# Two more score steps ahead of the outputs in each row of a burst, three sums of w_out by DMA, and a new list of shifts and engines, in a lightning-attention and feed-forward kernel

## The chip, the cores and the metric

One NeuronCore of a Trainium2 chip runs the whole program. The metric is device time in microseconds, the median of several runs of the same program. PE is the matrix engine (PEld is its loading of weights, which overlaps its products), DVE, ACT and POOL are the three engines for elementwise work, SP is the engine that here only issues DMAs. PE writes to PSUM, of which there are eight banks; DVE and ACT read it, POOL does not here.

## The reference

Attention with a decaying state, over four batches, eight heads, 768 positions and a head size of 64, in blocks of 64 positions; then a feed-forward network with SiLU over all 3072 tokens (512 to 2048 and back).

```python
Dmask = np.where(rel >= 0, lam[:, None, None] ** rel[None, :, :], 0.0)
for b in range(nb):
    qb, kb, vb = (q[:, :, sl], k[:, :, sl], v[:, :, sl])
    intra = np.einsum('bhic,bhjc->bhij', qb, kb) * Dmask[None]
    intra = np.einsum('bhij,bhjd->bhid', intra, vb)
    inter = np.einsum('bhid,bhde->bhie', qb * lam_pow[None], kv_state)
    out[:, :, sl] = intra + inter
    kb_dec = kb * rev_pow[None]
    kv_state = lam_block[None, :, None, None] * kv_state + np.einsum('bhsd,bhse->bhde', kb_dec, vb)
...
h = x @ w_in
g = h * (1.0 / (1.0 + np.exp(-h)))
return (g @ w_out)
```

## The kernel before

**Units.** The kernel works on blocks of 128 positions of one batch (24 units, all eight heads at once); two units make a pair, so there are 12 pairs (numbered 0 to 11), three to a batch. For a pair, `load_pair` (L432) fetches k, q and v as three transfers of 512 KB into `raw`; `prepare` casts k and q to bf16 (`kq`, four casts in pairs 4 to 11, of 64 partitions each), scales v by powers of lambda (`vd`), and turns `kq` to `kqT`, by PE in pairs 0 to 3 (L578) and by a transposing DMA on SP's queue (L593) from pair 4 on. `attention` makes the states (`y`, `xf`, and `xs_all`/`xe_all` as bf16 copies that PE can read) and the masks over the scores (`st`).

**Bursts.** From pair 3 on the small matmuls of a pair are issued in one burst, made of 64x64 tiles of the PE array; a matmul in the upper row of tiles and one in the lower run side by side, and the function `burst` keeps a list for each row (0 and 1) and merges the two by estimated time. A burst of pair n holds up to four kinds of step: the **states' terms** of pair n-1 (L633, `inter64`: queries times the carried state), the **states** of pair n (L659, "d", one chunk at a time in each row), the **scores** of pair n (L670, "s"), and the **outputs** of pair n-1 (L626, "o": masked scores times v). States, scores and outputs have eight steps in each row (four pairs of heads, two halves), of two matmuls each; the states' terms have four in each row. Outputs are added in PSUM to the states' terms, which went to the same banks from other rows of the array; so ahead of the first output stands a fence (`fence(at_inter)`): a `nop` of PE that waits until the last of the states' terms is done. In the kernel before, the order in a burst that has both a new and an old pair is: row 0: states' terms, states (chunk 0), outputs, scores; row 1: states' terms, four score steps, outputs, states (chunk 1, unless the pair ends a batch), the other four score steps. The burst is cut into three parts (after the last output, after the last score of the first two pairs of heads, end), so that DVE can start the evacuation `xt` and the masks `st` early. Bursts of pairs 5 to 11 have both an old pair that is in `CROSSED` and a new one.

**Feed-forward.** `product1` (L935) multiplies a group of units with w_in, ACT applies SiLU (L951, `g`), and `product2` (L977) multiplies by w_out for units 0 to 11. Units 12 to 23 go in fours: `product2_of_four` (L1126) uses a seven-product scheme for 2x2 blocks, and so does `product1_of_four` (L1254) for the fours from units 16 and 20. These need sums of quarters: of `g` (`asum`, tag "a"; some by a copy on SP's queue, L1107, and an accumulating DMA on POOL's queue, L1113), of w_out (`bsum`, tag "b", made by `sums_of_w_out` from five pairs of quarters, two halves each), of x (`xsum`) and of w_in (`wsum`, tag "w"). `bsum` and `wsum` live in slots of the pool `raw` (13 slots), as do the loads.

**The order of everything.** Nothing is issued in the order of the program text. Each piece of work is added to a `Planner` as a task with a key, costs by engine that may do it, dependencies and buffers; the planner plays the program forward with these costs, takes on each free engine the ready task with the lowest key whose buffers are free, and the tasks are then issued in the resulting order, which on each engine is fixed from then on. Keys are about twice the pair's number; loads have keys from -100 up, transposes -150 up, the copies for `bsum` by DMA would have `TKEY + i / 4 - 2` (i is the place in the dictionary `SEVEN`, whose order is 3, 4, 5, 1, 2, 7, 6) with `TKEY` 9. Two dictionaries adjust it: `SHIFT` adds to the key of a task or of a family of tasks (by its tag: `('first', 6)` are all first products of group 6), and `HOME` pins a task to one engine. Among the constants, `AWAY` lists the pairs whose casts and scalings may also go to POOL, and `BMOVED` the products whose sums of w_out are made by DMA: a copy of 512 KB on SP's queue (`put`) and an accumulating DMA of 512 KB on POOL's (`more`), in place of two additions on DVE or POOL. Up to 19 us, gaps on PE are filled with products of `ones` (L1321).

Of the kernel before, what the change touches and what calls it, by code (L numbers as in the profile page):

```python
# [39 lines left out]
def names_of(tag):  # L40


    if not isinstance(tag, tuple):
        return tag, None, None
    kind, n = tag[:2]
    if kind in ("cast", "scale", "burst", "mask", "y", "xe", "xf", "xt"):
        whole = "pair", n
    elif kind in ("first", "silu", "x", "to u", "u2", "u3", "h12", "h22"):
        whole = "group", n
    elif kind in ("seven", "a", "a copy", "to P", "to B", "to R", "on R", "m3", "c11", "c12", "c21", "c22"):  # L50
        whole = "four", n
    else:
        whole = None
    return tag, tag[:2] if len(tag) > 2 else None, whole


class Planner:
# [5 lines left out]
    BEGIN = {"PE": 0.8, "ACT": 5.6, "DVE": 2.7, "POOL": 3.4, "SP": 0.8}  # L63
    SWITCH = 0.095

    SHIFT = {('cast', 10, 1, 0): -0.5, ('cast', 10, 1, 1): -2.5, ('cast', 6): -3.5, ('cast', 7, 1, 0): -1.5, ('first', 2): -0.5,
             ('first', 2, 6): -8, ('first', 3, 6): -8.5, ('first', 4, 4): 1, ('first', 5, 0): -4, ('first', 5, 6): -0.5,
             ('first', 6): 6.25, ('first', 6, 11): 2.25, ('first', 6, 12): -1, ('first', 6, 14): 13.25, ('first', 6, 15): 2.25,
             ('first', 6, 2): 0.5, ('first', 6, 3): 0.25, ('first', 6, 4): -4.5, ('first', 6, 5): -10.75, ('first', 7): -0.25,
             ('first', 7, 0, 4): 1.75, ('first', 7, 1, 4): 1, ('first', 7, 2, 3): 1, ('first', 8, 0, 5): -4,  # L70
             ('first', 8, 1, 1): -3.5, ('first', 8, 2, 4): 4.5, ('four', 12): 4.5, ('four', 20): -0.75, ('group', 2): 0.25,
             ('group', 3): -5.5, ('group', 7): 4.75, ('group', 8): -7.5, ('load w', 3, 1): -1.5, ('mask', 11): 5.75, ('mask', 5): 3,
             ('mask', 7, 0, 1): 3, ('mask', 8, 0, 0): 5.75, ('mask', 9, 0, 1): 0.25, ('outputs', 0, 0): 4, ('pair', 10): 2.5,
             ('pair', 11): -9.75, ('pair', 4): -7.5, ('pair', 5): -0.75, ('pair', 9): 8.75, ('scale', 3, 0): -1, ('score', 1): 8,
             ('second', 10): 7, ('seven', 12): 0.5, ('seven', 12, 3): -8.25, ('seven', 12, 5): -4.75, ('seven', 16): 3.75,
             ('seven', 20): 3.75, ('silu', 8, 1, 0, 1): 2.75, ('states', 2, 0): 6.75, ('store', 9): -2, ('turn', 3, 0, 1): -10.75,
             ('turned', 1): -7.25, ('u3', 8): 5.5, ('w', 1): 6.75, ('xe', 0, 0, 1): 4.5, ('xe', 11): 11.75, ('xe', 3, 0, 0): 1.5,
             ('xf', 6): -10.25, ('xt', 7, 1): 7, ('y', 10, 0, 0): 5.75}
    HOME = {('a', 16, 1, 1): 'POOL', ('a', 20, 5, 0): 'POOL', ('a', 20, 5, 1): 'POOL', ('b', 3, 1): 'POOL',
            ('cast', 11, 1, 1): 'POOL', ('cast', 3, 0, 1): 'ACT', ('cast', 4, 0, 0): 'DVE', ('cast', 5, 0, 0): 'POOL',  # L80
            ('cast', 5, 1, 0): 'POOL', ('cast', 5, 1, 1): 'ACT', ('cast', 6, 0, 0): 'DVE', ('cast', 6, 1, 0): 'DVE',
            ('cast', 6, 1, 1): 'ACT', ('cast', 7, 1, 0): 'DVE', ('cast', 7, 1, 1): 'ACT', ('cast', 8, 1, 1): 'DVE',
            ('cast', 9, 0, 0): 'POOL', ('cast', 9, 1, 0): 'POOL', ('cast o', 1, 1): 'DVE', ('cast o', 2, 0): 'ACT',
            ('cast o', 2, 1): 'ACT', ('cast w', 1, 3): 'POOL', ('m3', 12): 'DVE', ('result', 1): 'ACT', ('scale', 11, 0): 'POOL',
            ('scale', 9, 0): 'POOL', ('to u', 7, 3): 'DVE', ('turned', 0, 0, 1): 'DVE', ('turned', 0, 1, 0): 'ACT',
            ('u3', 8, 0): 'DVE', ('u3', 8, 1): 'ACT', ('u3', 8, 2): 'ACT', ('w', 3, 0): 'POOL', ('w', 4, 0): 'POOL',
            ('x', 7, 3): 'POOL', ('x', 8, 1): 'POOL', ('xe', 6, 0, 0): 'POOL', ('xe', 6, 0, 1): 'POOL', ('xe', 7, 0, 0): 'ACT',
            ('xf', 10, 0, 1): 'POOL', ('xf', 4, 0, 1): 'DVE', ('xf', 7, 0, 0): 'POOL'}
    FIRST, LAST, AHEAD = {"SP": 1.15, "ACT": 1.15, "POOL": 1.0}, 1.0, 0.75

    def __init__(self, pools, becomes):
# [5 lines left out]
    def add(self, key, on, fn, deps=(), bufs=(), nbytes=0, kind=None, prior=(), late=0.0, tag=None, lock=False):  # L97
        key = key if isinstance(key, tuple) else (key,)
        key = (key[0] + sum(self.SHIFT.get(n, 0.0) for n in names_of(tag) if n is not None),) + key[1:]
        if tag in self.HOME:  # L100
            on = {self.HOME[tag]: on[self.HOME[tag]]}
        t = Task(key, on, fn, deps, list(bufs), nbytes, kind, prior, late)
# [183 lines left out]
def kernel(  # L286
# [11 lines left out]
    B, H, S, D = q.shape  # L298
# [4 lines left out]
    NP = H // 2  # L303
# [3 lines left out]
    EARLY = 4  # L307
    FINE = (0,)
    TIED, SOLO, CROSSED = 3, (3,), range(4, 12)
    AWAY, XAWAY, OWN = range(5,12), (), (0, 1)  # L310
    PORT = 3
    SMALL = (0, 1)
    OKEY = 0.0
    WKEY, WCAST, WON = -2.0, {"POOL": 0.75, "ACT": 0.62, "DVE": 0.45}, [("POOL", "ACT", "DVE")] * 2 + [("POOL", "DVE"), ("POOL", "ACT")]
    FIRST_ONES, ONES_UNTIL = 10, 19.0
    BMOVED, POOLED = (), (6,)
    LOADED, MOVED, HEAD = (4, 9), (12,16), (1.8, 1.8, 1.2, 0.6)
    TKEY, SEVENS, LAG, WSKEY, FIRST_SEVENS = 9.0, 12, 5.0, 14.0, (16,20)

    ctx.enter_context(tc.manual_schedule())  # L320
    const = ctx.enter_context(tc.tile_pool(name="const", bufs=1))
# [157 lines left out]
    xt = [Buf(f"xt{len(us)}") for us in groups]  # L479
# [123 lines left out]
    def burst(n, alone=False):  # L603
# [3 lines left out]
        o, new = dict(last_pair), n < NU // 2 and not alone  # L607
# [38 lines left out]
        if new:  # L646
            kq, kqT, vd, ck, cv, turned, kq_of, t_of = ready_of[n]
# [28 lines left out]
        def queue(row, what, width, fn, *more, part=slice(None)):  # L676
            rows[row].extend([(what, 0.0005 + 0.00044 * width, lambda a=(k, r) + more: fn(*a), k) for k, r in steps][part])
# [2 lines left out]
            queue(0, "d", 64, state, 0)  # L680
        if o:

            ahead = NP if new and o["n"] in CROSSED else 0
            if new:
                queue(1, "s", 128, score, 1, part=slice(ahead))
            queue(0, "o", 128, output, 0)
            queue(1, "o", 128, output, 1)
        elif new:
            queue(1, "s", 128, score, 1)
        if new:  # L690
            if not final:
                queue(1, "d", 64, state, 1)
            queue(0, "s", 128, score, 0)
            if o:
                queue(1, "s", 128, score, 1, part=slice(ahead, None))
        order, at = [], [0.0, 0.0]
        while rows[0] or rows[1]:
            c = 0 if rows[0] and (not rows[1] or at[0] <= at[1] + 1e-9) else 1
            what, w, f, k = rows[c].pop(0)
# [30 lines left out]
    def attention(n):  # L730
# [10 lines left out]
        if tied:  # L741
            if n - 1 in SOLO:
                burst(n, True)
            buf, sts, bursts = burst(n)
            de = bursts[1]
# [556 lines left out]
    for n in range(NU // 2):  # L1302
        attention(n)
    burst(NU // 2)
    if FIRST_SEVENS:
        sums_of_w_in()
# [17 lines left out]
    ends, first = {}, {}  # L1324
# [9 lines left out]
    def vacant(a, z):  # L1334

        best = None
        for b in {(b.pool, b.slot): b for _, b in first.values()}.values():
            spans = sorted(lives[b.pool, b.slot])
            if all(end + 0.3 < a or start >= z - 1e-6 for start, end in spans):
                nxt = min([start for start, _ in spans if start >= z - 1e-6], default=1e9)  # L1340
                if best is None or nxt < best[0]:
                    best = nxt, b
        return best and best[1]

    at = 0.0
    for start, _, e, t in planned:
        if e == "PE":
            if not at:
                occupy(vacant(0.5, start), FIRST_ONES, 512)
            elif start < ONES_UNTIL and start - at > 0.15:  # L1350
                b = vacant(at, start)
# [34 lines left out]
```

## Time and profile before

| what | value |
|---|---|
| median of 3 runs (lowest, highest) | 205.16 us (204.65, 205.41) |
| the profiled execution, whole | 204.5 us |
| its span, first to last instruction | 202.8 us |
| granted PE clock, mean | 0.998 |
| L935 PE, first products | 67.4 us busy, 448 matmuls |
| L977 PE, second products | 49.6 us busy, 192 matmuls |
| casts to kq: DVE, ACT, POOL | 18, 17 and 13 in pairs 4 to 11 |
| bsum additions on DVE | 9 of 128x1024, mean 1081 ns |
| bsum additions on POOL | 1, 2549 ns |

The span is what the profiler sees between the first and the last instruction; the device time has some 1.7 us more around it. Busy time of PE includes the pipelined ends of its matmuls; the spacing of their starts tells how fast PE really runs. The trace shows the first products from 16.52 us on, without a break from 17.93 us; the first burst at 39.26 us and the last at 143.54 us; the last matmul ends at 199.67 us.

### The profile page before, as it was taken

The page shows a single profiled execution, that of the slowest core. Times are in us where ns is not written, and L with a number is a line of the kernel's source. Part 1 is how long each engine was busy: PE and PEld are TensorE (multiplying, and loading weights), DVE is VectorE, ACT ScalarE, POOL GpSimd, SP SyncE. Part 2 cuts the span into 40 slices and gives each one's busy share as a digit, 9 for nine tenths or more (in the row PEclk, how much of TensorE's full clock was granted, in tenths as well). Part 3 has the DMA queues.
Part 4 walks back from the last instruction along what each step waited for, and adds up shares of the span by engine and source line. Part 5 has one row for each costly group of instructions (what it writes and reads, how often), then busy time and mean ns, then how long its engine had stood idle before and what let it go on. Part 6 is the DMA issues. An engine that isn't in the chain of part 4 may idle for free.

```text
span 202.8 us, 6082 instructions
## 1 busy us (share of the span) xinstructions
PE 196.8 (97%) x2585; PEld 145.3 (72%) x2585; DVE 146.2 (72%) x231; ACT 123.4 (61%) x193; POOL 71.4 (35%) x84
## 2 busy tenths in 40 slices
PE   6999999999999999999999999999999999999993
PEld 2776887867865557557776465458888888888882
DVE  3697749778994949599795875969765766743972
ACT  3697887849785655705384626683796878564010
POOL 4105430222560400058766041338954372000800
PEclk9999999999999999999999999999999999999999
DMA  4999999999999999899999471119997967111324
GB/s 110 339 335 366 386 362 334 368 313 382 230 282 261 318 344 298 208 311 218 303 255 213 130 128 33 57 58 222 176 184 184 218 179 136 52 55 52 107 103 155
DMA packets 71658, 44.43 MB, mean 219 GB/s; under 512 B 18448, under 2 KB 64528, under 8 KB 71632
## 3 DMA queue, kind: packets, MB, share of 16 engines
q1 hardware_dynamic: 62400, 34.74, 62.4%
q0 software_dynamic: 5456, 4.46, 14.4%
q10 hardware_dynamic: 3776, 4.86, 7.2%
q8 instruction: 20, 0.33, 0.6%
q14 instruction: 6, 0.05, 0.1%
HBM read 27.27 MB, written 6.29 MB: 165 GB/s over the span
## 4 chain that ended last, share of the span: by engine, by line
PE 90%; DVE 5%; issue 2%; ACT 1%; ACTq 0%
PE banks L935 27%; PE banks L1126 18%; PE banks L977 17%; PE banks L1254 12%; PE banks L1321 4%; PE banks L626 2%; PE banks L670 2%; PE banks L578 2%; DVE kq L409 1%; DVE xt L414 1%; PE banks L633 1%; DVE st L414 1%; PE banks L659 1%; PE banks L848 1%; PE banks L898 1%
## 5 line engine op out<-in xcount | busy, mean ns | idle before, releaser
L935 PE MATMUL banks<-xt,w_in_bf 128*128 128x256 bf16 (+1 forms) x448 | 67.4, 288 | 0.4 <-DVE xt L414 0.2
L951 ACT ACTIVATE g<-banks 128x512 bf16<-128x512 f32 x64 | 46.0, 745 | 26.8 <-PE banks L935 25.4
L935 PEld LDWEIGHTS <-w_in_bf 128*128 128x128 bf16 x448 | 42.9, 98 | 15.3 <-issue 0.8
L977 PE MATMUL banks<-w_out_bf,g 128*128 128x512 bf16 x192 | 49.6, 379 | 0.0
L414 DVE TENSOR_TENSOR st<-banks,tri 128x512 bf16<-128x512 f32 (+1 forms) x42 | 29.9, 757 | 3.7 <-PE banks L670 2.9
L977 PEld LDWEIGHTS <-g 128*128 128x128 bf16 x192 | 18.3, 98 | 19.1
L414 DVE TENSOR_TENSOR xt<-banks,lam_xe 128x512 bf16<-128x512 f32 x24 | 16.0, 684 | 12.5 <-PE banks L626 12.3
L1126 PE MATMUL banks<-bsum,g 128*128 128x256 bf16 x160 | 21.2, 273 | 0.0
L407 ACT ACTIVATE kq<-raw 64x512 bf16<-64x512 f32 (+3 forms) x24 | 18.5, 799 | 2.7 <-DMA raw<-in_k_dram 1.2
L407 ACT ACTIVATE osb<-banks 128x512 f32<-128x512 f32 (+1 forms) x15 | 8.7, 582 | 17.5 <-PE banks L977 12.2
L1126 PEld LDWEIGHTS <-asum 128*128 128x128 bf16 x176 | 17.2, 98 | 2.0
L409 DVE CAST kq<-raw 64x512 bf16<-64x512 f32 (+3 forms) x21 | 15.2, 741 | 4.0 <-DMA raw<-in_k_dram 2.5
L1126 PEld LDWEIGHTS <-g 128*128 128x128 bf16 x160 | 15.6, 98 | 1.9
L414 POOL TENSOR_TENSOR xf<-y,lam_be 128x256 f32<-128x256 f32 (+1 forms) x11 | 8.2, 749 | 22.1 <-DVE y L789 21.9
L1017 DVE TENSOR_TENSOR asum<-g 128x1024 bf16<-128x1024 bf16 x11 | 9.1, 836 | 8.3 <-PE banks L1126 2.9
L1270 ACT ACTIVATE g<-tmp 128x512 bf16<-128x512 f32 x16 | 12.4, 774 | 3.5 <-DVE tmp L1017 3.3
L1017 DVE TENSOR_TENSOR tmp<-banks,tmp 128x512 f32<-128x512 f32 x16 | 11.0, 687 | 4.8 <-PE banks L1254 4.1
L414 DVE TENSOR_TENSOR vd<-raw,lam_v 128x1024 bf16<-128x1024 f32 (+1 forms) x11 | 12.3, 1120 | 3.0 <-DMA raw<-in_v_dram 2.9
L1254 PE MATMUL banks<-xsum,wsum 128*128 128x256 bf16 x96 | 14.4, 273 | 0.0
L1017 POOL TENSOR_TENSOR asum<-g 128x1024 bf16<-128x1024 bf16 x3 | 6.4, 2121 | 22.8 <-PE banks L1126 19.1
L1254 PEld LDWEIGHTS <-wsum 128*128 128x128 bf16 x128 | 12.4, 98 | 1.5
L1321 PE MATMUL banks<-ones 128*128 128x128 bf16 (+1 forms) x85 | 11.0, 277 | 1.9 <-DVE ones L358 1.5
(96 smaller groups left out, 294.6 us busy)
## 6 DMA issues: line engine op xcount, KB each, us to landing
raw<-in_k_dram SPq DMA_DIRECT2D x11, 512.0 KB, 5.4
raw<-in_q_dram SPq DMA_DIRECT2D x11, 512.0 KB, 6.1
raw<-in_v_dram SPq DMA_DIRECT2D x11, 512.0 KB, 7.6
out_dram<-osb ACTq DMA_DIRECT2D x18, 256.0 KB, 3.6
raw_w<-in_moe_w_in_dram SPq DMA_DIRECT2D x8, 512.0 KB, 8.0
raw_w<-in_moe_w_out_dram SPq DMA_DIRECT2D x8, 512.0 KB, 6.6
asum<-g SPq DMA_DIRECT2D x8, 256.0 KB, 2.6
asum<-g POOLq DMA_DIRECT2D x8, 256.0 KB, 5.1
```

What stands on the lines that cost most here:

```text
L407: nc.scalar.activation(o, i, AF.Copy)
L409: nc.vector.tensor_copy(o, i)
L414: (nc.vector if e == "DVE" else nc.gpsimd).tensor_tensor(o, a, b, op=AL.mult)
L578: nc.tensor.transpose(t[:, r, m, :], kq_of()[:, i, r, 2 * m:2 * m + 2, :], ident)
L935: nc.tensor.matmul(t[:, j, :], lhsT=w_in_bf[:, ko, 128 * m:128 * m + 128], rhs=xt[gi].tile[:, ko, :], start=(ko == 0), stop=(ko == KI - 1))
L951: nc.scalar.activation(t.rearrange("p j (c a r) -> p (j c) r a", c=n // U, r=2), psum_of(bank).rearrange("p (jc r a) -> p jc r a", r=2, a= ...
L977: nc.tensor.matmul(psum_of(bank), lhsT=gs[gi, ko][1](1, 128 * gp, 128)[:, 0], rhs=w_out_bf[:, ko], start=(ko == 0), stop=(ko == KO - 1))
L1017: (nc.vector if e == "DVE" else nc.gpsimd).tensor_tensor(o, x, y, op=op)
L1126: nc.tensor.matmul(part(bank, u), lhsT=lhs(u), rhs=b_of(ko), stop=ko == 7, skip_group_check=True, start=opens and not ko and not u)
L1254: nc.tensor.matmul(two_of(bank)[:, f], lhsT=(wb[0].tile if wb else w_quarter(*wl))[:, ko, fs], rhs=(xsum(xr) if isinstance(xr, int) else x ...
L1270: nc.scalar.activation(t.rearrange("p j (c a r) -> p (j c) r a", c=2, r=2), src().rearrange("p (jc r a) -> p jc r a", r=2, a=64), AF.Silu)
L1321: nc.tensor.matmul((t if b.pool == "bank" else t[:, 0])[:, 0:w], lhsT=ones[:, 0:128], rhs=ones[:, 0:w], start=True, stop=True)
```

## The change

It has three parts. In `burst`, where a new pair and an old pair of `CROSSED` meet, the order becomes: row 0: states' terms, states, two score steps, outputs, the other six score steps; row 1: states' terms, six score steps, outputs, states, the other two. All steps stay. `AWAY` becomes empty, so that casts go to DVE or ACT and scalings to DVE alone, and `BMOVED` becomes (1, 7, 6), so that three of the five sums of w_out are made by DMAs. `SHIFT` and `HOME` are replaced by new lists, of which some lines follow.

```diff
-    SHIFT = {('cast', 10, 1, 0): -0.5, ('cast', 10, 1, 1): -2.5, ('cast', 6): -3.5, ('cast', 7, 1, 0): -1.5, ('first', 2): -0.5,
...
-             ('pair', 11): -9.75, ('pair', 4): -7.5, ('pair', 5): -0.75, ('pair', 9): 8.75, ('scale', 3, 0): -1, ('score', 1): 8,
-             ('second', 10): 7, ('seven', 12): 0.5, ('seven', 12, 3): -8.25, ('seven', 12, 5): -4.75, ('seven', 16): 3.75,
-             ('seven', 20): 3.75, ('silu', 8, 1, 0, 1): 2.75, ('states', 2, 0): 6.75, ('store', 9): -2, ('turn', 3, 0, 1): -10.75,
...
-    HOME = {('a', 16, 1, 1): 'POOL', ('a', 20, 5, 0): 'POOL', ('a', 20, 5, 1): 'POOL', ('b', 3, 1): 'POOL',
...
-            ('cast', 9, 0, 0): 'POOL', ('cast', 9, 1, 0): 'POOL', ('cast o', 1, 1): 'DVE', ('cast o', 2, 0): 'ACT',
-            ('cast o', 2, 1): 'ACT', ('cast w', 1, 3): 'POOL', ('m3', 12): 'DVE', ('result', 1): 'ACT', ('scale', 11, 0): 'POOL',
-            ('scale', 9, 0): 'POOL', ('to u', 7, 3): 'DVE', ('turned', 0, 0, 1): 'DVE', ('turned', 0, 1, 0): 'ACT',
-            ('u3', 8, 0): 'DVE', ('u3', 8, 1): 'ACT', ('u3', 8, 2): 'ACT', ('w', 3, 0): 'POOL', ('w', 4, 0): 'POOL',
...
+    SHIFT = {('a', 20): -0.75, ('cast o', 1, 3): -0.25, ('cast o', 2, 3): -7.25, ('first', 2, 3): -6.75, ('first', 2, 5): -2.75,
...
+             ('group', 8): 3, ('load w', 3, 1): -1.5, ('mask', 10, 0, 1): 9.5, ('mask', 11): 4, ('mask', 7, 0, 0): 6.25,
+             ('mask', 9): 9, ('on R', 20, 0): 0.25, ('pair', 10): -12, ('pair', 11): -11.25, ('pair', 7): -10.5,
+             ('scale', 3, 0): -1, ('scale', 8, 0): -2, ('score', 2): 9, ('score', 2, 1): -4, ('second', 0): 2.25,
...
+    HOME = {('a', 12, 1, 0): 'POOL', ('a', 20, 2, 0): 'POOL', ('a', 20, 5, 0): 'POOL', ('a', 20, 7, 0): 'POOL', ('c12', 16): 'DVE',
...
+            ('u2', 7, 1): 'DVE', ('w', 1, 0): 'DVE', ('w', 4, 0): 'POOL', ('x', 8, 1): 'POOL', ('xe', 10, 0, 0): 'POOL',
+            ('xe', 6, 0, 1): 'ACT', ('xe', 9, 0, 1): 'POOL', ('xf', 10, 0, 0): 'DVE'}
...
-    AWAY, XAWAY, OWN = range(5,12), (), (0, 1)
+    AWAY, XAWAY, OWN = (), (), (0, 1)
...
-    BMOVED, POOLED = (), (6,)
+    BMOVED, POOLED = (1, 7, 6), (6,)
...
-            ahead = NP if new and o["n"] in CROSSED else 0
+            ahead = (2, NP + 2) if new and o["n"] in CROSSED else (0, 0)
             if new:
-                queue(1, "s", 128, score, 1, part=slice(ahead))
+                queue(0, "s", 128, score, 0, part=slice(ahead[0]))
+                queue(1, "s", 128, score, 1, part=slice(ahead[1]))
             queue(0, "o", 128, output, 0)
             queue(1, "o", 128, output, 1)
...
-            queue(0, "s", 128, score, 0)
+            queue(0, "s", 128, score, 0, part=slice(ahead[0] if o else 0, None))
             if o:
-                queue(1, "s", 128, score, 1, part=slice(ahead, None))
+                queue(1, "s", 128, score, 1, part=slice(ahead[1], None))
```

## The prediction

> **What bounds the kernel now.** I read the page's busy times first, then the chain of waits, then the idle time of PE stretch by stretch, and last the bursts that the change rewrites.
>
> ```profile
> span 202.8 us, 6082 instructions
> ...
> PE 196.8 (97%) x2585; PEld 145.3 (72%) x2585; DVE 146.2 (72%) x231; ACT 123.4 (61%) x193; POOL 71.4 (35%) x84
> ...
> PE 90%; DVE 5%; issue 2%; ACT 1%; ACTq 0%
> ```
>
> PE is busy for 97% of the span and holds 90% of the chain that ended last. A busy PE need not be a fast one, so I took the spacing of matmul starts: a 128x256 product (L935, L1126, L1254) comes every 0.109 us and a 128x512 one (L977) every 0.217 us, at a granted clock of 0.998, from 17.7 us to 199.67 us. What exceeds that spacing in these 182 us is a fixed 0.09 us ahead of each burst, the insides of the bursts, and one true wait, at 90.45 to 91.9 us (0.38 + 0.28 = 0.66 us). So only three things can shorten the span: less PE time in the bursts, that wait, and the ends (before 17.7 us, where PE fills time with ones until w_in has landed at 15.80 and 17.04 us and is cast; and some 3 us of last copy and store). The load sequence and the last stores are not edited, so I put the ends at no change.
>
> **The bursts, the part that the diff writes out.** The timeline of the burst at 74.30 us (L633 the states' terms, L659/L670 states and scores, L626 the outputs), and then that of the last burst, in which nothing stands between the two:
>
> ```profile
> 74.30 0.42 PE L633 MATMUL banks<-kqT,xs_all 64*64 64x128 bf16 x16
> ...
> 74.73 0.23 PE L659 MATMUL banks<-vd,kq 64*64 64x64 bf16 x4
> 74.85 0.51 PEld L626 LDWEIGHTS <-vd 64*64 64x64 bf16 x32
> 74.88 0.64 PE L626 MATMUL banks<-st,vd 64*64 64x128 bf16 x32
> ```
>
> ```profile
> 143.54 0.42 PE L633 MATMUL banks<-kqT,xs_all 64*64 64x128 bf16 x16
> ...
> 144.10 0.51 PEld L626 LDWEIGHTS <-vd 64*64 64x64 bf16 x32 [0.30 <-issue]
> 144.13 0.64 PE L626 MATMUL banks<-st,vd 64*64 64x128 bf16 x32 [0.17 <-PE banks L633]
> ```
>
> In both the outputs' first weight load comes 0.55 us after the first states' term, whether 24 to 40 matmuls stand between or none: the fence on the last of the states' terms sets it, and that term's modelled end (74.72; 143.96) lies 0.13 us before. Matmul by matmul, in the first burst: the last state matmul ahead of the fence starts at +0.469 us; the next could start about 0.028 us on (the spacing before it), at +0.497; the first output starts at +0.583. The exposed wait is 0.086 us. In the seven bursts that hold both kinds (74.30, 87.28, 96.85, 107.47, 116.52, 125.16, 135.51) it is 0.086, 0.111, 0.072, 0.085, 0.085, 0.072, 0.085: **0.60 us in all**.
>
> The change puts two score steps of each row there. What two steps a row take is read from the tail of the 96.85 burst, where 16 score matmuls (four steps in each row) last 0.23 us: 0.114 us for two. The output would then be free to start at +0.611 us, 0.028 after the fence opens: the wait is covered, and the same 0.114 us is gone from the tail. The gain is the exposed wait, 0.086 us a burst, 0.60 us in all; eight score matmuls and their weight loads move per burst, none is added or dropped. Side effects: xt on DVE waits for the last output, which comes 0.028 us later; the first masks wait for row 0's fourth score step, which comes 0.086 us earlier. Bounds: 0 (the fence moves along with the extra work) and 0.80 (seven times 0.114). I take 0.60, measured in place.
>
> A rule that speaks against it: the Trainium skill (TensorE: Matmul & The Clock Gate, "Single matmul latency") puts a lone warm matmul at (398 + N)/2.4 ns, which for N = 128 gives 0.219 us; by it the last states' term, started at +0.202, is over at +0.421, before +0.497, and there would be no wait to cover: gain 0. The trace agrees with the duration (its modelled 0.216 us) but the weight load comes 0.13 us later still, in the last burst with nothing else to blame.
>
> **The constants.** AWAY empty: casts and scalings of pairs 5 to 11 may not run on POOL. There it did 10 casts of 64x512 at 0.81 us, 3 of 64x1024 at 1.25 and 2 scalings at 1.90: 15.6 us. The scalings become DVE's (2 x 1.22 = 2.4 us); the casts take 6.3 us if all go to DVE (0.42 and 0.69 each, undisturbed) or 9.3 if all go to ACT (0.62 and 1.05). BMOVED (1, 7, 6): six DVE additions of w_out quarters (1.08 each, 52 to 61 us) go, 6.5 us, and three copies of 512 KB on SP's queue with three accumulating DMAs of 512 KB on POOL's come. Neighbours: the 256 KB copies of asum land 0.8 us apart, the accumulating ones 1.45 to 1.5 us apart; so 3 x (1.6 + 2.95) = 13.6 us of all DMA engines. Their place follows from the keys: a copy (7.75 to 8.5) and a load (-100 up) want the same raw slots, so the copies stand behind the last load (issued at 106.24 us). Each accumulation waits on POOL's queue for its copy to land, with the xf and xs products behind it, and the next burst's states' terms wait for those; the products that need the sums begin after 137.18 us. The stages between:
>
> ```profile
> core 0: us, PE busy (x) PEld busy (x) DVE busy (x) ACT busy (x) POOL busy (x), PEclk, DMA share, GB/s
> ...
> 92.00:105.00 13.00, 13.00 (x193) 10.10 (x193) 11.66 (x20) 7.45 (x11) 10.66 (x13) 1.00 1.20 247
> 105.00:120.00 15.00, 15.00 (x268) 8.55 (x266) 10.75 (x18) 7.41 (x11) 5.42 (x5) 1.00 0.75 169
> 120.00:137.00 17.00, 17.00 (x265) 9.00 (x262) 13.02 (x22) 11.25 (x17) 4.79 (x7) 1.00 0.28 67
> ```
>
> DMA has 0.25 x 15 + 0.72 x 17 = 16.0 us free from 105 to 137, POOL 21.8: the 13.6 us are hidden. If that cover is gone, they push transposes and A sums (rival C). Three raw slots less are held from 53 to 106 us, one pair's loads; PE waits for no load there, so nothing is booked for it.
>
> **The lists** (SHIFT, HOME) have no row of their own: they reorder the same instructions and choose engines. Best case: the one wait of PE goes, -0.66 us. What it comes from:
>
> ```profile
> 86.32 3.95 DVE L409 CAST kq<-raw 64x1024 bf16<-64x1024 f32 x3
> 87.50 2.14 POOL L1017 TENSOR_TENSOR wsum<-w_in_bf 128x1024 bf16<-128x1024 bf16 x1
> 90.30 0.69 DVE L414 TENSOR_TENSOR xt<-banks,lam_xe 128x512 bf16<-128x512 f32 x1
> 91.05 2.18 PE L935 MATMUL banks<-xt,w_in_bf 128*128 128x256 bf16 x16 [0.22 <-DVE xt L414]
> ```
>
> Of the three casts one took 2.92 us against 0.42 for its like, ending just after POOL's sum does: while POOL works on SBUF, DVE stands still; xt behind it on DVE came late, and PE waited. Worst case: such a stall of 2.50 us with no cover, at one burst +2.5, or 0.66 at each of several. I take 0, nearest to what 182 us of the present order show, and keep -0.66 and +2.5.
>
> **Sum.** -0.60 (bursts) + 0 + 0 = -0.60. The profiled execution took 204.5 us around its span of 202.8; it would take 203.9. It lies 0.66 below the median of the runs shown, 205.16, from which I count: **204.6 us**.
>
> **Rivals.**
> A. The lists also remove the wait at 90 us: 204.56 - 0.66 = 203.9. For it: the pin of sum ('w', 3, 0) on POOL is gone, and with 15.6 us less on POOL there are fewer such stalls. Against: ('w', 4, 0) stays there, and four A sums (2.12 us each) instead of three are pinned to POOL.
> B. Slower: DVE overflows. From 92 to 105 us it is busy 11.66 of 13 us, 1.34 free, and POOL's two scalings and nine of its casts lie between 92 and 120. Once more than 1.34 us of that lands on DVE ahead of xt, each burst there repeats the wait of 0.66 us; with the three bursts of 92 to 120: 204.56 + 1.98 = 206.5. Against: ACT has 5.55 us free in the same stretch, and a POOL at rest gives DVE back up to 0.43 us for each of its 64x512 casts (mean 0.85, alone 0.42).
> C. The new DMAs collide: issued before 105 us, where the DMA share is 1.0 and more, they delay transposes by up to 13.6 us. These land 5.8 to 12.7 us ahead of their bursts, mostly about 10.2: 13.6 - 10.2 = 3.4, so 208.0. Against: the order by keys.
> D. The burst gains nothing, since the fence moves along: 205.2. For it only the rule above; against it the last burst's 0.55 us.
>
> **How the numbers follow.** Forecast 0.39, A 0.25, B 0.18, C 0.10, D 0.08. Of no change a measurement here can tell about 0.5%, 1.03 us: faster means below 204.1, slower above 206.2. Faster: most of A (0.21) and the forecast's lower edge (0.05), 0.26. Slower: most of B (0.16), C (0.10), the forecast's upper edge (0.02), 0.28. The rest, 0.46, is neither. The range runs from 203.4 (A with the burst's upper bound and a little) to 206.9 (B with some spread), leaving out C and the edges; the forecast's own is 204.0 to 205.3.
>
> **What would show it.** Right: outputs' weight load in the seven bursts still about 0.55 to 0.58 us after the first states' term with no gap before it, each burst about 0.09 us shorter; three 512 KB DMAs of POOL between 105 and 137 us; no cast to kq and no vd on POOL; PE idle no more than about 0.7 us from 18 to 199. Wrong: PE waits for xt or xs behind casts on DVE (B), for kqT or a late sum (C), or a first output that moves out with the added scores beyond +0.62 us (D).

## The result, and the profile after

| | before | after |
|---|---|---|
| median of 22 runs (lowest, highest), us | 204.62 (204.46, 205.41) | 205.39 (204.63, 206.59) |
| ratio to before, 95% interval | | 1.0034 [1.0021, 1.0048] |
| profiled span, us | 202.8 | 203.5 |
| last matmul ends, us | 199.67 | 200.12 |
| the seven rewritten bursts, sum, us | 11.30 | 10.54 |

The change made the kernel 0.77 us slower, where 0.60 us less was forecast. The page of the changed kernel:

```profile
span 203.5 us, 6078 instructions
...
PE 195.7 (96%) x2586; PEld 144.2 (71%) x2586; DVE 137.8 (68%) x234; ACT 130.0 (64%) x200; POOL 57.8 (28%) x71
...
PE 72%; DMA 14%; SPq 6%; POOL 3%; ACT 2%; issue 1%; DVE 0%; POOLq 0%
```

PE has less busy time than before (195.7 against 196.8 us), DVE and POOL too, and still the span grew: the chain that ended last is no longer almost all PE. DMA, absent before, holds 14% of it: 7% are the load of w_out, 4% the sums of g, 3% the load of w_in. The same burst as in the prediction, on PE and its weight loads:

```profile
74.03 0.42 PE L629 MATMUL banks<-kqT,xs_all 64*64 64x128 bf16 x16
...
74.51 0.30 PE L666 MATMUL banks<-kqT 64*64 64x128 bf16 x8
74.64 0.64 PE L622 MATMUL banks<-st,vd 64*64 64x128 bf16 x32
75.08 0.53 PE L666 MATMUL banks<-kqT 64*64 64x128 bf16 x16
75.55 0.39 PE L974 MATMUL banks<-w_out_bf,g 128*128 128x512 bf16 x1
```

```profile
74.61 0.51 PEld L622 LDWEIGHTS <-vd 64*64 64x64 bf16 x32
```

Eight score matmuls now stand where PE had waited; the outputs start 0.61 us after the first of the states' terms (0.58 before), and the burst is over after 1.52 us instead of 1.60. All seven are shorter. The wait of 0.66 us at 90 us is gone too: no row of PE waits for DVE's xt any more. What came instead, on PE, and the piece of the chain that leads to it:

```profile
143.73 1.04 PE L1251 MATMUL banks<-xsum,wsum 128*128 128x256 bf16 x8
146.07 1.05 PE L1123 MATMUL banks<-w_out_bf,asum 128*128 128x256 bf16 x8 [1.31 <-DMA asum<-g]
```

```profile
135.29 2.62 POOL asum L1110 x2
137.91 0.35 POOL g L1110
138.25 7.77 DMA asum<-g
146.03 0.05 issue
146.07 1.05 PE banks L1123 x8
```

The fifth product of the four from unit 12 needs a sum of quarters of g that an accumulating DMA makes. It was issued at 138.25 us, behind three others on POOL's queue, and landed at 146.03; by the spacing of its products PE would have begun at 144.60. That is 1.47 us of nothing on PE. A second, smaller wait stands at 48.4 us (0.41 us in two pieces), where a second product waits for the cast of a half of w_out:

```profile
48.88 0.59 PE L974 MATMUL banks<-w_out_bf,g 128*128 128x512 bf16 x2 [0.21 <-ACT w_out_bf L403]
```

The account for the end of the last matmul: bursts -0.76, wait at 90 us -0.66, wait for the sum +1.47, waits for w_out +0.41: +0.46, and +0.45 is measured. That it comes out so well is partly luck, since two terms that nearly cancel are left out of it. The first products run without a break from 18.27 us instead of 17.93 (the first two pieces of w_in landed at 16.32 and 17.56 us instead of 15.80 and 17.04), +0.34; the small matmuls between 18 and 40 us, placed differently, take 0.36 us less.

Two more amounts lie behind the last matmul and outside the span. From the end of the last matmul to the end of the span it is 3.42 us instead of 3.12: between the landing of the last store and its drain, SP takes six `EVENT_SEMAPHORE` instructions, 0.06 us apart, where it took one before. And the device time is longer than the span of the same execution by 1.99 to 2.11 us, against 1.66 to 1.78 in the runs of the kernel before that list both. Each of these 0.3 us stands in every run below that has the new lists and constants, whatever else it changes, and in none that has the old ones. So 0.63 us of the change stands at the ends, where no order on PE reaches it; which of the lists or constants brings it is open. In the profiled pair 0.45 + 0.30 + 0.33 make 1.08 us, the distance from 204.5 to 205.58; the medians differ by 0.77.

### The profile page after: what moved, and what is told of

It reads as the page before. It is cut to its first block, busy times and chain, and to the rows that moved or that the text cites. A ratio compares the mean times of both kernels' runs of the same rounds, so it can differ in the third digit from the quotient of the medians.

```text
span 203.5 us, 6078 instructions
## 1 busy us (share of the span) xinstructions
PE 195.7 (96%) x2586; PEld 144.2 (71%) x2586; DVE 137.8 (68%) x234; ACT 130.0 (64%) x200; POOL 57.8 (28%) x71
## 4 chain that ended last, share of the span: by engine, by line
PE 72%; DMA 14%; SPq 6%; POOL 3%; ACT 2%; issue 1%; DVE 0%; POOLq 0%
PE banks L932 21%; PE banks L974 19%; PE banks L1123 16%; PE banks L1251 10%; DMA raw_w<-in_moe_w_out_dram 7%; SPq L428 4%; DMA asum<-g 4%; DMA raw_w<-in_moe_w_in_dram 3%; PE banks L666 2%; PE banks L622 2%; POOL asum L1110 1%; PE banks L629 1%; SPq L447 1%; POOL asum L1014 1%; ACT g L948 1%
## 5 line engine op out<-in xcount | busy, mean ns | idle before, releaser
L932 PE MATMUL banks<-xt,w_in_bf 128*128 128x256 bf16 (+1 forms) x448 | 63.7, 288 | 0.4 <-POOL w_in_bf L407 0.2
L948 ACT ACTIVATE g<-banks 128x512 bf16<-128x512 f32 x64 | 45.7, 742 | 21.5 <-PE banks L932 19.2
L974 PE MATMUL banks<-w_out_bf,g 128*128 128x512 bf16 x192 | 47.8, 379 | 0.2 <-ACT w_out_bf L403 0.2
L403 ACT ACTIVATE kq<-raw 64x512 bf16<-64x512 f32 (+3 forms) x35 | 25.4, 755 | 2.6 <-ACT osb L403 0.9
L403 ACT ACTIVATE osb<-banks 128x512 f32<-128x512 f32 (+1 forms) x13 | 7.5, 578 | 16.8 <-PE banks L974 8.7
L410 POOL TENSOR_TENSOR xf<-y,lam_be 128x256 f32<-128x256 f32 (+1 forms) x11 | 6.7, 612 | 39.3 <-DVE y L786 38.8
L410 DVE TENSOR_TENSOR vd<-raw,lam_v 128x1024 bf16<-128x1024 f32 (+1 forms) x13 | 14.9, 1145 | 3.2 <-DMA raw<-in_v_dram 3.2
L405 DVE CAST kq<-raw 64x512 bf16<-64x512 f32 (+3 forms) x23 | 13.1, 588 | 4.2 <-DMA raw<-in_k_dram 2.6
L1267 ACT ACTIVATE g<-banks 128x512 bf16<-128x512 f32 x16 | 11.8, 740 | 6.1 <-PE banks L1251 5.8
L1123 PE MATMUL banks<-w_out_bf,asum 128*128 128x256 bf16 x96 | 13.1, 273 | 1.3 <-DMA asum<-g 1.3
L1110 POOL DMA_DIRECT2D asum<-g x8 | 9.7, 1268 | 12.4 <-DMA asum<-g 5.4
```

The costliest lines, as they stand in the source:

```text
L403: nc.scalar.activation(o, i, AF.Copy)
L405: nc.vector.tensor_copy(o, i)
L410: (nc.vector if e == "DVE" else nc.gpsimd).tensor_tensor(o, a, b, op=AL.mult)
L932: nc.tensor.matmul(t[:, j, :], lhsT=w_in_bf[:, ko, 128 * m:128 * m + 128], rhs=xt[gi].tile[:, ko, :], start=(ko == 0), stop=(ko == KI - 1))
L948: nc.scalar.activation(t.rearrange("p j (c a r) -> p (j c) r a", c=n // U, r=2), psum_of(bank).rearrange("p (jc r a) -> p jc r a", r=2, a= ...
L974: nc.tensor.matmul(psum_of(bank), lhsT=gs[gi, ko][1](1, 128 * gp, 128)[:, 0], rhs=w_out_bf[:, ko], start=(ko == 0), stop=(ko == KO - 1))
```

## The experiments

In all these kernels the plan was left as it was, and only what is issued was changed: a step moved in the planned order, or another order of the burst's steps issued under the old cost. So every instruction that is not named stands in its place on its engine.

**The bursts alone, in either kernel.** Here `merged` builds the burst's steps with so many score steps ahead in each row; `order` goes into the costs of the plan, `issued` into the program.

```diff
+    PLANNED, ISSUED = (0, NP), (2, NP + 2)
...
+        order, cuts = merged(PLANNED)
+        issued, parts_at = merged(ISSUED)
```

> The kernel before with the new order of steps issued in its seven bursts, and nothing else changed on any engine. Theory N (the bursts gain, the new list loses it): each of the seven bursts 0.08 to 0.11 us shorter, time 0.6 to 0.8 us under before (ratio about 0.9965). Rival B (the burst's order itself costs, for instance through later outputs or masks): no gain or a loss, ratio 1.000 or more.

Measured: 204.11 us against 204.66, ratio 0.9972 [0.9959, 0.9985]; the seven bursts last 10.52 us. The gain in time, 0.55 us, is less than the 0.78 of the bursts; in this profile the wait for xt behind the casts has grown from 0.66 to 0.77 us, so 0.11 us of it was lost there. In the changed kernel the two orders are exchanged:

> The changed kernel with the old order of steps issued in its seven bursts, every other order kept. Theory N: what list and constants cost by themselves, 0.77 + 0.76 = about 1.5 us over before (1.0 to 2.0; ratio about 1.0075). Rival B: at or under the changed kernel, ratio 1.0035 or less.

Measured: 206.24 us, ratio 1.009 [1.0058, 1.0122]; the bursts last 11.32 us, PE's wait for the sum is 1.27 us. The new order of the burst is a gain in both kernels, and lists and constants cost about 1.6 us by themselves (1.2 to 2.5 by the interval, of six runs), 0.63 of it at the ends.

**Are the added DMAs to blame?**

```diff
                 def more(e, b=b, qs=qs):
-                    nc.gpsimd.dma_start(out=b.tile, in_=b_quarter(*qs[1]), accum_op=AL.add)
+                    pass
```

> The changed kernel without the three accumulating DMAs of 512 KB on POOL's queue that finish the sums of w_out: their copies remain, the second operand is left out of the sums 1, 6 and 7, so the output differs. The order on PE, DVE, ACT and SP is the same. Rival T (the added DMAs make the A sums of the four from unit 12 late): PE's wait of 1.47 us at about 144.5 us falls below 0.5 us, time 0.2 us or more under before. Theory N (the list puts the fifth product right behind the DMA that makes its sum): the wait stays between 1.0 and 1.8 us, time 0.3 to 1.0 us over before.

Measured: 204.77 us, ratio 1.0011 [0.9996, 1.0026]. The row of PE in question, of this kernel:

```profile
144.92 1.05 PE L1123 MATMUL banks<-w_out_bf,asum 128*128 128x256 bf16 x8 [1.10 <-DMA asum<-g]
```

Without the three DMAs the wait is still there, 1.26 us by the spacing. The time, 0.11 us over before, is what neither theory expected: N had 0.3 to 1.0 over, T 0.2 under. In the profile the last matmul ends 1.15 us earlier than in the changed kernel, and 0.94 of this is there at the first of the seven bursts already (73.09 us instead of 74.03): no wait at 48 us, and an earlier start. The left-out DMAs, issued from 115 us on, can't touch that. The other 0.21 us is what the wait lost. So the wait isn't theirs, and the profiles show nothing else that they cost.

**The order of the sums.** In the planned order, one of POOL's DMAs goes behind two others:

```diff
+    later(("a", 12, 7, 0), ("a", 12, 2, 1))
```

> The changed kernel with one accumulating DMA on POOL's queue moved: that of the seventh product's first half, for the four from unit 12, goes behind those of the fifth and second products. All else is in the same order. Theory N: the fifth product's second sum lands about 1.45 us earlier, PE's wait at about 144.5 us falls to 0 to 0.4 us and the time to 0.2 to 0.8 us under before (ratio about 0.997). Rival T: the wait stays over 1 us, since the queue is late as a whole.

Measured: 203.37 us (five runs), ratio 0.9938 [0.9927, 0.995], a larger gain than expected. POOL and then PE of this kernel:

```profile
134.25 2.62 POOL L1110 DMA_DIRECT2D asum<-g  x2
138.02 1.28 POOL L1110 DMA_DIRECT2D asum<-g  x1 [1.15 <-DMA asum<-g]
140.17 1.28 POOL L1110 DMA_DIRECT2D asum<-g  x1 [0.87 <-ACT banks L403]
140.92 5.76 POOL L1110 DMA_DIRECT2D g<-g  x4
```

```profile
142.97 1.04 PE L1251 MATMUL banks<-xsum,wsum 128*128 128x256 bf16 x8
143.84 1.04 PE L1123 MATMUL banks<-w_out_bf,asum 128*128 128x256 bf16 x8
```

The sum is the third DMA instead of the fourth, lands at 143.53 us, 0.3 us before it is needed, and the product follows its predecessor with no idle time. One DMA's place in one queue was the whole wait. Not all of the time comes from it: of the 2.24 us by which the last matmul ends earlier, 0.76 is there at the first of the seven bursts, where this DMA has no part. The same kernel once more:

> The same kernel as e4_sums_in_time, to compare with e11 on one chip and to see whether its time stands: 203.2 to 203.7, no wait of PE at 144 us.

Measured: 203.97 us (203.17 to 205.88), ratio 0.997 [0.9945, 0.9995], PE's wait for the sum 0.03 us (the sum landed just in time). The wait stays away; the time is above the 203.2 to 203.7 that were expected. Its profile, taken of an execution of 205.36 us, shows most of the reason in PE's row at 50 us:

```profile
50.08 0.59 PE L974 MATMUL banks<-w_out_bf,g 128*128 128x512 bf16 x2 [0.94 <-ACT w_out_bf L403]
```

The half of w_out that this product needs landed at 49.37 us in this execution, at 48.18 in the first profile after and at 47.06 in that of e4; the waits are 1.10, 0.38 and 0 us by the spacing. Of the 2.0 us by which its last matmul ends later than in e4's profile, all but 0.03 us stands before the first of the seven bursts (75.24 us instead of 73.27). The changed order stands close behind that load, and executions differ in it. The changed kernel itself, a second time:

> The changed kernel once more, for a second profile. Theory N: PE's wait for the fifth product's second sum stands again at about 144 us, 1.0 to 1.8 us; waits before 60 us come and go with the landing of the loads; time 0.4 to 1.0 us over before. Rival (the wait was of one execution): under 0.5 us at that place.

Measured: 205.37 us, ratio 1.0025 [1.0005, 1.0045]; waits of 1.19 us for the sum and 0.15 for w_out. The wait for the sum is in every profile of this order (1.47, 1.19, and 1.27 and 1.26 in e2 and e3), that for w_out comes and goes.

**Is a late sum bad as such?** The kernel before, its fifth product's second sum put behind the two of the seventh:

```diff
+    later(("a", 12, 5, 1), ("a", 12, 7, 1))
```

> The kernel before with the accumulating DMA of the fifth product's second half, for the four from unit 12, moved behind the two of the seventh product on POOL's queue, so that it lands about 2.9 us later. Theory N (what counts is how far behind the sum its product stands on PE; in the order of before that is several us): no new wait of PE, time within 0.3 us of before. Rival (a late sum costs as such): a wait of 1 us or more at 144 to 152 us and as much in time.

Measured: 205.05 us against 204.70, ratio 0.9999 [0.9979, 1.0018] (the ratio is not the quotient of the two medians, and its interval leaves room for 0.4 us either way). The sum lands at 151.83 us instead of 146.42, and there is no new wait:

```profile
152.39 0.38 PE L1254 MATMUL banks<-xt,w_in_bf 128*128 128x256 bf16 x2
152.61 1.91 PE L1126 MATMUL banks<-w_out_bf,asum 128*128 128x256 bf16 x16
```

The same product in the kernel before:

```profile
151.26 1.91 PE L1126 MATMUL banks<-w_out_bf,asum 128*128 128x256 bf16 x16
```

The order before has it at 151.26 us and needs the second sum at 152.13, 5.7 us behind its landing; in this run 1.7 us are left. (Its profile has a wait of 1.3 us at 20.8 us as well, for a load of w_in that landed at 21.49 us and not at 19.73; POOL's DMAs at 141 us have no part in that.)

**The wait at 90 us.** It is gone in the changed kernel; this run asks what made it. In the kernel before, one sum of w_in goes from POOL to DVE, behind xt:

```diff
+    later(("w", 3, 0), ("xt", 5, 1))
+    planned = [(s, n, "DVE" if t.tag == ("w", 3, 0) else e, t) for s, n, e, t in planned]
```

> The kernel before with one addition of w_in quarters (the third sum's first half, 128x1024) moved from POOL, where it stood at 87.5 us, to DVE, behind the two evacuations xt of the burst at 87.28 us. Nothing else is moved. Theory L (POOL's work on SBUF held DVE's cast up, 2.92 us against 0.42, so xt came late and PE waited): the cast takes 0.4 to 0.7 us, PE's waits at 90 to 92 us (0.66 us) fall below 0.1, time 0.4 to 0.7 us under before (ratio about 0.997). Rival: DVE is too full there anyway, the waits stay over 0.4 us and the time within 0.2 us of before.

Measured: 204.02 us against 204.80, ratio 0.9968 [0.995, 0.9986]. DVE of this kernel:

```profile
86.43 1.46 DVE L409 CAST kq<-raw 64x1024 bf16<-64x1024 f32 x3
88.69 0.69 DVE L414 TENSOR_TENSOR xt<-banks,lam_xe 128x512 bf16<-128x512 f32 x1 [0.80 <-PE banks L626]
```

The three casts take 1.46 us instead of 3.95; xt now waits for PE, not PE for xt, and PE's wait at 90 us is gone. This shows the cause of the wait in the kernel before. In the changed kernel it need not be what removed it, for there xt comes later still, behind four masks:

```profile
87.73 2.48 DVE L410 TENSOR_TENSOR st<-banks,tri 128x512 bf16<-128x512 f32 x4 [2.47 <-PE banks L666]
91.60 0.68 DVE L410 TENSOR_TENSOR xt<-banks,lam_xe 128x512 bf16<-128x512 f32 x1
```

That is 5.3 us behind the start of its burst, where it was 3.0 before. PE has other products to do until its next burst, at 94.61 us, and needs this xt only behind that.

**Both gains in the kernel before.**

> The kernel before with the new order of steps in its seven bursts and that addition moved off POOL, its list and constants otherwise. If both gains stand and add: 0.55 + 0.55 = about 1.1 us under before (0.8 to 1.4; ratio about 0.9945). If one covers the other (PE arrives at the same late data): 0.5 to 0.7 us under.

Measured: 203.24 us (202.91 to 203.84), ratio 0.9923 [0.9895, 0.995]: 1.56 us under before, somewhat more than the 0.8 to 1.4 that were expected. This beats both kernels; its profile shows no wait of PE between 18 and 199 us but the fixed 0.09 us ahead of each burst.

**How much the fence has to give.** On the kernel of e4, the old order of the burst:

> The changed kernel with the seventh product's accumulating DMA moved, and the old order of steps in its seven bursts. PE has no wait left there behind which a gain could hide, so this measures the bursts alone: Theory N: 0.6 to 0.8 us over the kernel with the new order (203.37). Rival (part of the gain in the bursts is given back at later waits for data): 0.4 us or less over it.

Measured: 204.62 us, ratio 0.9983 [0.9963, 1.0003]. That is 1.25 us over the first timing of e4 and 0.65 over its second; the bursts last 11.32 us against 10.54, 0.78 more, and this profile has 0.28 us of the wait for w_out. And with four steps ahead:

> The changed kernel with the seventh product's accumulating DMA moved, and four score steps instead of two ahead of the outputs in either row of the seven bursts. Theory N (two steps just cover the fence's wait): outputs start later by the added work, about 0.11 us, bursts are as long as with two steps within 0.03 us, time within 0.2 us of the kernel with two. Rival (each step put ahead is worth the same): seven times 0.1, about 0.7 us under it.

This kernel, as built, issued part of its outputs and scores twice (608 output matmuls instead of 384), since the cut behind the first scores came ahead of the one behind the outputs. Its 212.61 us say nothing of the question. Mended:

```diff
         issued, parts_at = merged(ISSUED)
+        parts_at[1] = max(parts_at[:2])
```

> As e7_four_steps_in_e4 was meant: the changed kernel with the seventh product's accumulating DMA moved and four score steps ahead of the outputs in either row, each step issued once. Theory N: outputs start about 0.11 us later, bursts as long as with two steps within 0.03 us each, time within 0.2 us of the kernel with two (203.37). Rival (each step put ahead is worth the same): about 0.7 us under it.

Measured: 204.43 us (203.21 to 206.02), ratio 0.9985 [0.9957, 1.0013]: over the 203.37 that either theory counted from, and not to be told from e12's 203.97. The bursts tell more: outputs start at 0.63 to 0.70 us instead of 0.57 to 0.61, and the seven last 10.43 us against 10.54. Two steps cover the wait but for 0.1 us in all; two more move the outputs out by the work that they add.

## Why the prediction was wrong, point by point

- **The bound.** Right in the main: PE without gaps, so that burst time, true waits and the ends count. One term was missing, the small matmuls between 18 and 40 us: placed differently, they took 0.36 us less.
- **The bursts, -0.60.** Right in mechanism, a little small: -0.76 in the profiles, near the bound of 0.80 that I gave; e1 shows -0.55 in the median [-0.84, -0.31]. The outputs moved out by no more than 0.03 us, since the eight added score matmuls took only 0.09 us ahead of the fence where I had read 0.114 from the tail. Rival D falls: the outputs' weight load comes 0.53 to 0.58 us after the first states' term in the new order as well, and the wait was there to be covered. What falls with it is not the rule's duration of one matmul, which these runs don't measure (the 0.216 us of the trace is a modelled end), but the step from that end to the opening of the fence.
- **The constants, 0.** The copies went where the keys said, behind the last load (103.34 us): the first was issued at 110.99 us, the accumulations between 115.6 and 120.7 us. The copies landed 1.55 and 1.66 us apart, as counted (1.6). The accumulations were slower: the last landed at 132.15 us, 16.5 us after the first was issued, where I had 8.9 for the three; PE did not wait for the sums of w_out. Rival C in its form with late transposes didn't happen: the last landed at 124.97 us for the burst at 134.58. The sign that I gave for it, a late sum, did come, but without its cause: without the three accumulations PE waits for it all the same, 1.26 us (e3). Rival B didn't happen either: DVE was busy 12.03 of the 13 us from 92 to 105, ACT 10.40, and no burst waited for xt.
- **The lists, 0: the step that failed.** I took 0, between a gain of 0.66 us and a loss of up to 2.5, because the order before had shown little waiting; but what holds for the waits of the old order did not hold for the new one. The gain of 0.66 came, as in rival A. The cause that I named is the right one for the wait (e5), but by the rows shown there the new order of PE, which needs that xt later, would have removed it too, and no run separates the two. And one wait of 1.47 us came at a place that I hadn't looked at. I had looked for room in engines and queues by stage, and there was room. What decided was how far behind one DMA its consumer stands on PE: 5.7 us in the old order, less than nothing in the new (e4, e10). With the waits for w_out, PE was idle for 2.2 us from 18 to 199 us (0.32 of it at 18 us), where I had allowed 0.7. The new lists drop the shifts of this very four, `('seven', 12)` and `('seven', 12, 5)`; but the planner made the order from lists and constants together, and no run tells their shares apart.
- **The ends, no change: failed too.** I put them at nothing because loads and last stores are not edited. What lies behind the last matmul and outside the span grew by 0.63 us all the same, in every run with the new lists and constants.
- **The level.** I counted from the median of three runs, 205.16 us; 22 runs give 204.62. This shifted the forecast up by 0.54 us and hid part of the miss: -0.60 was forecast and +0.77 came. That 205.39 us lies inside the range of 203.4 to 206.9 is luck, since its upper part was there for rival B, which didn't happen.

## What to carry to other kernels

When the bottleneck engine is full, a new order of the same work can lose more than a local change gains, as here; so list each transfer that the new order puts close ahead of its consumer, and measure the distance, not the load of the stage. If a change mixes a local gain with a new plan, time the two apart with the order of everything else held: here the parts were about -0.7 and +1.6 us, and moving one DMA turned the sum round. Put a queue of accumulating DMAs in the order in which its sums are needed: here that was worth 1.2 to 1.5 us of waiting. And compare what lies behind the last matmul and outside the span as well: here it was 0.63 us that no row of PE shows.

## What the runs showed of the hardware

- Accumulating DMAs of 256 KB within SBUF that stood in a row landed about 1.5 us apart, though they were issued 0.75 us apart (142.05, 142.80 and 143.56 us: landed 148.98, 150.51 and 151.99). The plain copies of the kernel before landed 0.73 to 0.85 us apart, issued 0.64 to 0.96 apart. A copy issued among the accumulations at 136.11 us took 4.64 us, two issued ahead of them 3.0 and 3.1; but one at 135.47 us took 2.50, so that the accumulations slow a copy down is not shown.
- A 64x512 cast on DVE took 2.92 us beside an addition of POOL, and the three casts of that group 1.46 in all once it was gone.
- The fence on PE costs the same whether no small matmul or up to 32 of them fill it: the next weight load comes 0.53 to 0.58 us after the first of 8 or 16 states' terms, in all these kernels, until the work between is longer than that (0.62 to 0.65 us with four steps).
- The same load of w_out landed between 46.5 and 49.4 us in twelve profiles, with nearly the same instructions ahead of it; it was issued between 39.9 and 41.9 us, so part of the spread is older than the load itself. An order that stands right behind it waits for it in some executions and not in others (0 to 1.15 us in the profiles). How much of the spread of the changed kernel's times (204.63 to 206.59 us) comes from it is not shown.
- Six `EVENT_SEMAPHORE` instructions of SP at the end of the program, instead of one, took 0.30 us more.
